# Attention with a joint block, routing and a second layer: two-strip values products, five places for bias groups, and copies at other steps

## The chip, the cores and the metric

The kernel runs on one core of a Trainium2 chip. The metric is the device time of one execution in microseconds (us). The kernel before takes 361.13 us, the median of three runs (360.67 to 361.41).

## The reference

Three layers follow one another: an attention whose scores get a bias from a small network of relative positions, a mixture of experts that sends each token to one of eight, and a gated layer. Inputs and output are 32-bit floats.

```python
B, H, S, D = 2, 8, 576, 64           # batches, heads, sequence, head width
scores = q @ k.transpose(0, 1, 3, 2) / sqrt(D)
x = log1p(abs(i - j)) / log1p(max(i, 1))
h = maximum(x[..., None] @ w1 + b1, 0)          # 32 hidden units per (i, j)
scores += (h @ w2).transpose(2, 0, 1)           # one bias plane per head, both batches share it
attn = softmax(scores) @ v
tokens = attn as 1152 rows of 512
expert = argmax(tokens @ w_gate); gate = softmax at that expert
y = gate * relu(tokens @ w1[expert]) @ w2[expert]   # at most 288 tokens per expert
h = y @ w_in                                    # 512 -> 2048
out = (h * cos(h)) @ w_out
```

## The kernel before, in words

**Attention** is cut into nine blocks of 128 query rows and each block into four steps, one for a pair of heads: 36 steps. The 576 rows of a batch are four blocks of 128 and one of 64; the two blocks of 64 (one of each batch) are worked on together as the joint block, `BOTH`, which is the fifth in the order and holds steps 16 to 19.

All engines' orders are written out by hand, in `step_of(n)`. Step n issues the score products of step n+1 (`emit_qk`, L403, into the two-bank tiles `sa` and `sb`), and in the same step VectorE adds the bias and takes the row minimum of the negated score (`emit_sum`, L411; `mn`). ScalarE takes the exponential (`emit_exp`, L420), TensorE turns it in strips of 64 (`emit_tr`, L428), ScalarE copies the turned strips out of PSUM (`emit_tev`, L451 and L454). TensorE multiplies the turned strips of step n-1 with the values (`emit_pv`, L470), and ScalarE copies that product (L480). Two steps later the product is turned back (L501, L553 in the routing part) and scaled (L508).

`emit_pv` has the values as the stationary operand, in strips of 32 columns, and the turned exponentials as the moving one, so four strips lie side by side in the array. For a block of 128 rows that is 5 times 4 matmuls with 128 moving columns. For the joint block it is 2 times 5 times 4 with 64 moving columns. The trace shows each of these matmuls as two pairs of a weight load and a matmul.

**The bias** is made in 36 groups of 16 query rows, ten (`LEAD`) ahead of the first step and one in each of the steps 0 to 25, group g = n + 10 in step n. A group is: four hidden tiles `h` (`bias_h`, L321 on VectorE or L319 on ScalarE), two half products in `bb` of four strips each (`bias_half`, L347), two evictions on ScalarE into a place `ev_t[g]` (L353), and a copy from that place to the plane of its block (`bias_out`: L328 to `keep` or `bias`, L338 to `joint`, which lies in `wi`). The second half's eviction is done at the start of the next step. The places are three buffers taken in turn, `ev_buf[g % 3]`; only groups 8 to 13 have six of their own (`ev_first`). A place is written again only when the copy out of it has landed. `h` in step 0 is all four tiles of group 10, behind the first four sums.

**SP's queue** issues nearly all copies, one after the other, in the order in which they are written: bias copies, the queries (`fetch_q`, L306), the filling of the dispatch table with rows that count for nothing (`fill_rows`, L840, at the steps `FILL_AT`), zeros into the output (`fill_out`, L843, at `OUT_AT`), and `double` (L835), which copies the joint block's bias planes of a head pair to the second batch's 64 rows, once per step from step `DOUBLE_AT` on. A `double` waits for the bias copies of groups 16 to 19.

**Routing** runs inside the steps. After the first blocks the kernel picks the expert that it works on first and, at step `SECOND_CHOICE` on VectorE behind the step's scaling, the second one (`second_choice`: L684 and the four operations of `largest`, L674 to L677). SP reads that number two steps later. From step 26 on (`PLAIN`) there are no bias groups; VectorE then does parts of the weights' widening (L757 to L763). The experts and the gated layer come after step 35.

Of the kernel before, what the change touches and what calls it, by code (L numbers as in the profile page):

```python
# [20 lines left out]
B, H, S, D = 2, 8, 576, 64  # L21
# [6 lines left out]
RW = DM + 4  # L28
# [10 lines left out]
MAGS = 28, 29, 30, 31, 33  # L39
LOWS = {28: 3, 29: 2, 30: 2, 31: 3, 32: 2, 35: 3}  # L40
ROUTE_FROM = 17
FILL_AT = 6, 7, 8, 9, 13, 14, 15, 16, 17, 18, 19
DOUBLE_AT = 10
OUT_AT = 10, 12, 12, 20, 20, 21, 21, 22, 22
SECOND_CHOICE = 27
PLAIN = 26
LATE_FROM = 32
LATE_A = {33: 1}
# [5 lines left out]
LEAD = 10  # L54
# [13 lines left out]
BOTH = B  # L68
# [38 lines left out]
def attention_moe_kernel(  # L107
    ctx: ExitStack, tc: tile.TileContext,
    qd, kd, vp, small, ttab, wg, mw1, mw2, win, wout, out, dbg=None,
# [72 lines left out]
    cut = lambda a, n: flat[:, a:a + n]  # L182
# [2 lines left out]
    base = 9 * RW + 2 * NP * 128  # L185
    lt_buf = cut(base, 128)
    ev_buf = [cut(base + 144 + S * i, S) for i in range(3)]
    ev_first = dict(zip(range(8, 14), ev_buf + [cut(a, S) for a in (6 * RW + 60, S * 3, S * 2)]))
    v13 = cut(base + 144 + 3 * S, 640)


# [77 lines left out]
    bias_a = bias_p.tile([128, H, S], F32, name="bias0")  # L269
# [12 lines left out]
    def v_of(b, p, a, n):  # L282
        for lo, hi, t in v_parts[b, p]:
            if lo <= a and a + n <= hi:
                return t[:, a - lo:a - lo + n]
# [6 lines left out]
    def fetch_k(b, p):  # L292
        Y.dma_start(out=kt[b, p], in_=kd[b, :, 2 * p:2 * p + 2, :])
# [17 lines left out]
    def bias_h(g, on_act=(), quads=(0, 1, 2, 3)):  # L311
        _, _, first = GROUPS[g]
        for j in quads:
            base = first[j]
            h = h_lead[(4 * g + j) % 12] if g < LEAD else h_buf[(4 * g + j + 4) % 8]
            win_ = tt[:, C0 - base:C0 - base + S]
            col = pst[:, 4 * g + j:4 * g + j + 1]
            if j in on_act:
                A.activation(out=h, in_=win_, func=AF.Relu, bias=col, scale=1.0)  # L319
            else:  # L320
                V.tensor_scalar(out=h, in0=win_, scalar1=col, scalar2=0.0, op0=ALU.add, op1=ALU.max)  # L321
            h_t[g, j] = h

    ev_t = {}

    def bias_part(g, a, e):
        ib, r, _ = GROUPS[g]
        Y.dma_start(out=bias_t[ib][r:128:8][:, :, a:e], in_=ev_t[g][:, a:e])  # L328

    def bias_out(g, cuts=((0, S),)):  # L330
        ib, r, _ = GROUPS[g]
        ev = ev_t[g]
        if IBN[ib] == 128:
            for a, e in cuts:
                bias_part(g, a, e)
        else:
            for rr in range(2):
                Y.dma_start(out=joint[r + rr:64:8], in_=ev[64 * rr:64 * rr + 64])  # L338
        for j in range(4):
            h_t.pop((g, j))  # L340

    def bias_half(g, half, bank=bb):
        if half == 0:
            ev_t[g] = ev_first.get(g, ev_buf[g % 3])
        cols, ps = slice(half * 288, half * 288 + 288), bank[:, :288]
        for j in range(4):
            T.matmul(out=ps[32 * j:32 * j + 32, :], lhsT=w2s, rhs=h_t[g, j][:, cols], start=True, stop=True)  # L347

        def evict():
            if (g, half) == (NG - 1, 1):  # L350
                V.tensor_scalar(out=ev_t[g][:, cols], in0=ps, scalar1=rst[:, g:g + 1], scalar2=None, op0=ALU.mult)
            else:
                A.activation(out=ev_t[g][:, cols], in_=ps, func=AF.Copy, scale=rst[:, g:g + 1])  # L353
            if g == NG - 1:
                bias_part(g, half * 288, half * 288 + 288)
            elif half == 1:
                bias_out(g)

        return evict
# [1 line left out]
    lead_t = {}  # L361

    def bias_lead(g):
        ev_t[g] = bias_a[:, g] if g < 8 else ev_first[g]
        lead_t[g] = (xb, bb) if g == 9 else (t0, t1) if g % 3 == 2 else [s_bank[1 - g % 3][:, i] for i in range(2)]
        for half in range(2):
            for j in range(4):
                T.matmul(
                    out=lead_t[g][half][32 * j:32 * j + 32, 0:288], lhsT=w2s,
                    rhs=h_t[g, j][:, 288 * half:288 * half + 288], start=True, stop=True,  # L370
                )
# [11 lines left out]
    e_t, et_t, z_t, xs_t, xn_t, rz_t = {}, {}, {}, {}, {}, {}  # L383
# [76 lines left out]

    def emit_pv(n):
        b, ib, p = steps[n]
        et = et_t[n]
        et_t.pop(n)
        for c, a, e in [(c, 64 * c, 64 * c + 64) for c in range(B)] if b == BOTH else [(b, 0, 128)]:
            xo = sum_of(n)[:, a:e]
            for j in (4, 0, 1, 2, 3):
                for i in range(4):
                    u, at_ = i // 2, 512 + 32 * i if j == 4 else 64 * (4 * (i // 2) + j) + 32 * (i % 2)
                    T.matmul(  # L470
                        out=xo[32 * i:32 * i + 32], lhsT=v_of(c, p, at_, 32),
                        rhs=et[:, 4 if j == 4 else 5 * u + j, a:e], start=(j == 4), stop=(j == 3),
                    )
        if p == 0:
            xs_t[b, ib] = xs_buf[n // NP % 2]
            xn_t[b, ib] = rows[tile_of(b, ib)]
# [184 lines left out]
    def choose():  # L661
# [24 lines left out]

        hooks[SECOND_CHOICE, "values"] = [second_choice]
        hooks[SECOND_CHOICE + 2, "start"] = [lambda: known(ix2)]

# [99 lines left out]
    def warm(n):  # L789

        for _ in range(n):
            T.matmul(out=wu[:, 0:128], lhsT=ones, rhs=ones, start=True, stop=True)
# [60 lines left out]
            fetch_k(1, 0)  # L853
    load_v(0, (2,))
    fetch_k(1, 1)
    warm(8)
    emit_sum(0, 0)
    emit_sum(0, 1)
# [6 lines left out]
    def step_of(n):  # L865

        g, nxt = RUNS.get(n), RUNS.get(n + 1)
        at_step[0] = n
        if n > 1:
            b, ib, p = steps[n - 2]  # L870
            if p == NP - 1 and n < SOONER:
                finish_block(b, ib)
                ready.append((b, ib))

        while ready and n >= ROUTE_FROM:
            tile_done(*ready.pop(0))
        while late and n < LATE_FROM and late[0][0] == -2:
            whole(late.pop(0)[1])
        if 0 < n <= PLAIN:
            emit_exp(n, 1)  # L880
        while behind:
            behind.pop(0)()
        if n in MAGS:
            early_mags.pop(0)()
        hook(n, "first")
        if n + 1 < ns:
            b, ib, p = steps[n + 1]
            j = BLOCKS.index((b, ib))
            for u in range(2):
                emit_qk(n + 1, u)  # L890
            if p == 0 and 0 < j < len(BLOCKS) - 1:
                fetch_q(*BLOCKS[j + 1])
            if n == 0:
                bias_h(g)
            emit_exp(n + 1, 0)
        if n == ns - 4:
            aux[0] = V
        hook(n, "start")
        emit_tr(n)
        if n > 1:  # L900
            emit_nat(n - 2)
        hook(n, "turned")
        emit_tev(n, 2)
        if g is not None:
            bias_half(g, 0)()
        emit_tev(n, 0)
        if n >= LATE_FROM:
            go_on(run_late(LATE_A.get(n, 0)))
        emit_tev(n, 1)
        begun = run_late(LATE_B.get(n, n < LATE_FROM))  # L910
        e_t.pop(n)
        if nxt is not None:
            bias_h(nxt, quads=(0, 1))
        go_on(begun)
        if n > 1:
            emit_nrm(n - 2)
        if nxt is not None:
            bias_h(nxt, quads=(2, 3))
        while held:
            held.pop(0)()  # L920
        for _ in range(LOWS.get(n, 0)):
            early_lows.pop(0)()
        hook(n, "values")
        if 0 < n:
            emit_rz(n - 1)
            emit_pv(n - 1)
            if PLAIN <= n < ns - 1:
                emit_exp(n + 1, 1)
            emit_xs(n - 1)
        if n == SOONER:  # L930
            b, ib, p = steps[n - 1]
            finish_block(b, ib)
            tile_done(b, ib)
        go_on(run_late(LATE_C.get(n, 0)))
        if g is not None:
            evict = bias_half(g, 1, bb if n > 1 else xb[:, 128:])
            if g == NG - 1:
                evict()
            else:
                behind.append(evict)  # L940
        made_up()
        load_step(n)
        while again and again[0][0] <= n:
            fetch_piece(again.pop(0)[1])
        if n in FILL_AT:
            i = FILL_AT.index(n)
            fill_rows(256 * i, min(256, E1 * CAP - 256 * i))
        if 0 <= n - DOUBLE_AT < NP:
            double(n - DOUBLE_AT)
        for j, at_ in enumerate(OUT_AT):  # L950
            if at_ == n:
                fill_out(j)
        hook(n, "end")
# [139 lines left out]
    b, ib, p = steps[ns - 1]  # L1093
# [454 lines left out]
```

## Time and profile before

| | us |
|---|---|
| median of three runs | 361.13 (360.67 to 361.41) |
| the profiled execution, its own time | 361.79 |
| its span, first to last instruction | 360.0 |
| TensorE busy in the span | 341.8 (95%) |
| VectorE | 293.9 (82%) |
| ScalarE | 266.8 (74%) |
| GpSimd | 37.7 (10%) |

The mean granted TensorE clock is 0.994 of 2.4 GHz; the page's row of slices shows the full clock up to the last slice. Busy time of TensorE counts matmuls whose ends are modelled, so the shares say little of a single stage. What matters is which engine the others wait for in each step: a gap on TensorE, and what ended it.

### The profile page before, as it was taken

Reading aid. Unit: us, or ns where it says so; the run is one execution under the profiler, and the core shown is the slowest. Engines: PE = TensorE matmul, PEld = TensorE weight load, DVE = VectorE, ACT = ScalarE, POOL = GpSimd, SP = SyncE. Lnnn points to the kernel's source line nnn. Section 1 sums busy time; section 2 is a strip of 40 time slices with the busy share of each in tenths; the row PEclk is TensorE's granted clock in tenths of the full one; section 3 lists DMA queues with packets and bytes.
Section 4 is the critical chain, followed back from the end, with each engine's and each line's share of the span. In section 5 each row is a group of like instructions: output and inputs, shape, how many; then the busy total and the mean of one; then the engine's idle time right before and its main releaser. Section 6 shows DMA issues by size and latency. Waiting matters only on the chain. (4 is left out here: it accounts for less than half of the span.)

```text
span 360.0 us, 11244 instructions
## 1 busy us (share of the span) xinstructions
PE 341.8 (95%) x4459; PEld 272.8 (76%) x4459; DVE 293.9 (82%) x771; ACT 266.8 (74%) x627; POOL 37.7 (10%) x89
## 2 busy tenths in 40 slices
PE   7989999999989999898999999999999999999991
PEld 6346777775656777686789999968898898898880
DVE  5988889898869886988799999887997887876760
ACT  6768999987978898898943597387777667666560
POOL 3000001101001420110007112100000000000023
PEclk9999999999999999999999999999999999999997
DMA  7799966679976687799238698943243242110003
GB/s 234 203 246 278 251 168 194 203 157 258 277 244 190 205 247 192 249 258 310 90 109 309 167 353 280 295 157 119 66 121 107 91 131 73 58 62 0 2 28 117
DMA packets 47023, 63.89 MB, mean 177 GB/s; under 512 B 5772, under 2 KB 30476, under 8 KB 46962
## 3 DMA queue, kind: packets, MB, share of 16 engines
q1 hardware_dynamic: 45666, 60.24, 57.8%
q0 software_dynamic: 1152, 2.48, 1.9%
q8 instruction: 37, 0.61, 0.7%
q10 hardware_dynamic: 144, 0.36, 0.3%
q14 instruction: 24, 0.20, 0.2%
HBM read 41.08 MB, written 11.47 MB: 146 GB/s over the span
## 5 line engine op out<-in xcount | busy, mean ns | idle before, releaser
L420 ACT ACTIVATE e<-e,mn 128x576 f32<-128x576 f32 x72 | 56.2, 781 | 14.8 <-DVE mn L411 14.8
L321 DVE TENSOR_SCALAR h<-tt,sml 128x576 f32<-128x576 f32 x122 | 57.0, 513 | 0.1
L451 ACT ACTIVATE et<-t 128x512 f32<-128x512 f32 x72 | 38.7, 593 | 0.0
L347 PE MATMUL bb<-h,sml 128*32 128x288 f32 x400 | 35.6, 412 | 1.1 <-DVE h L321 0.6
L428 PEld LDWEIGHTS t<-ident,e 64*128 64x128 f32 x576 | 24.3, 139 | 8.9 <-issue 1.8
L403 PE MATMUL sb<-k,q 64*128 64x288 f32 (+1 forms) x160 | 27.0, 449 | 0.4 <-DVE lp L556 0.3
L353 ACT ACTIVATE wo<-bb,sml 128x288 f32<-128x288 f32 x49 | 24.7, 504 | 3.5 <-PE bb L347 2.1
L428 PE MATMUL t<-ident,e 64*128 64x64 f32 x576 | 26.1, 225 | 1.1 <-ACT e L420 0.8
L1281 PE MATMUL t<-yh,s1h 128*128 128x352 f32 (+1 forms) x88 | 26.8, 305 | 0.0
L1281 PE MATMUL t<-yh,s1l 128*128 128x352 f32 (+1 forms) x88 | 26.6, 303 | 0.0
L1281 PE MATMUL t<-yl,s1h 128*128 128x352 f32 (+1 forms) x88 | 26.5, 302 | 0.0
L1392 DVE TENSOR_TENSOR tn<-tn,kn 128x608 f32<-128x608 f32 (+2 forms) x18 | 13.0, 722 | 15.8 <-ACT kn L1389 15.7
L470 PE MATMUL sa<-et,wi 128*32 128x128 f32 (+1 forms) x800 | 23.0, 260 | 1.6 <-issue 1.6
L1402 ACT ACTIVATE gh<-tn 128x608 fp32r<-128x608 f32 (+2 forms) x18 | 11.8, 656 | 17.0 <-DVE tn L1399 17.0
L403 PE MATMUL sa<-k,q 64*128 64x288 f32 (+1 forms) x160 | 23.8, 406 | 0.0
L470 PEld LDWEIGHTS sa<-et,wi 128*32 128x32 f32 x800 | 19.5, 110 | 3.9 <-issue 1.7
L403 PEld LDWEIGHTS sb<-k,q 64*128 64x128 f32 (+1 forms) x160 | 10.5, 174 | 14.7 <-issue 6.0
L1018 PE MATMUL hp<-xh,s1h 128*128 128x288 f32 x64 | 19.5, 305 | 0.0
L1377 PE MATMUL hp<-s2h,gh 128*128 128x512 f32 x48 | 19.1, 399 | 0.0
L1021 ACT ACTIVATE hh<-hp 128x288 fp32r<-128x288 f32 x16 | 6.5, 409 | 17.0 <-PE hp L1018 17.0
L1377 PE MATMUL hp<-s2l,gh 128*128 128x512 f32 x48 | 19.0, 396 | 0.0
L1377 PE MATMUL hp<-s2h,gl 128*128 128x512 f32 x48 | 18.9, 394 | 0.0
(308 smaller groups left out, 999.9 us busy)
## 6 DMA issues: line engine op xcount, KB each, us to landing
keep<-win SPq DMA_DIRECT2D x16, 512.0 KB
keep<-wout SPq DMA_DIRECT2D x16, 512.0 KB
w1r<-mw SPq DMA_DIRECT2D x12, 512.0 KB
w2r<-mw SPq DMA_DIRECT2D x12, 512.0 KB
disp<-wo SPq DMA_DIRECT2D x10, 516.0 KB
bias<-wo SPq DMA_DIRECT2D x15, 288.0 KB
q<-qd SPq DMA_DIRECT2D x8, 512.0 KB
k<-kd SPq DMA_DIRECT2D x8, 288.0 KB
```

The source lines that it names most:

```text
L321: V.tensor_scalar(out=h, in0=win_, scalar1=col, scalar2=0.0, op0=ALU.add, op1=ALU.max)
L347: T.matmul(out=ps[32 * j:32 * j + 32, :], lhsT=w2s, rhs=h_t[g, j][:, cols], start=True, stop=True)
L353: A.activation(out=ev_t[g][:, cols], in_=ps, func=AF.Copy, scale=rst[:, g:g + 1])
L403: T.matmul(out=ps[a:e, half, 0:HS], lhsT=qt[b, ib][rows_, h, a:e], rhs=kt[c, p][rows_, u, :], start=True, stop=True)
L420: A.activation(out=e_t[n][:, u], in_=e_t[n][:, u], func=AF.Exp, scale=-1.0, bias=mn_t[n][:, u:u + 1], accum_out=z_t[b, ib][:, h:h + 1],)
L428: T.transpose(ps, src[half], ident[half, half])
L451: A.activation(out=et_t[n][:, 0:8, 64 * g:64 * g + 64], in_=halves[g], func=AF.Copy)
L470: T.matmul(out=xo[32 * i:32 * i + 32], lhsT=v_of(c, p, at_, 32), rhs=et[:, 4 if j == 4 else 5 * u + j, a:e], start=(j == 4), stop=(j == 3),)
L1018: T.matmul(out=ps, lhsT=a[g % 3][:, k], rhs=x[:, k], start=(k == 0 and i == 0), stop=(k == 3 and i == 2))
L1281: done.append(T.matmul(out=sums(f, i), lhsT=w[f % 3][:, k], rhs=ya[k][x][:, o0 + a:o0 + e], start=(k == 0 and n == 0), stop=(k == 3 and n ...
L1377: T.matmul(out=oacc[t][rows_of(t)], lhsT=x, rhs=b[f % 3], start=(f == 0 and n == 0), stop=(f == 15 and n == 2))
L1392: V.tensor_tensor(out=tn, in0=tn, in1=kn, op=ALU.subtract)
```

## The change

It has five parts.

1. `emit_pv` takes the joint block's values in two strips of 64 columns in place of four of 32: 20 matmuls a step in place of 40, each writing 64 rows.
2. Groups 14 to 26 take their places from five buffers in turn, `ev_buf` and two regions of `wo` that groups 12 and 13 used alone.
3. The copies are issued at other steps: one filling goes from step 13 to 10, three zero copies from steps 10, 12, 12 to 8, 9, 11, and the four `double`s from steps 10 to 13 to steps 12 to 15.
4. Two of group 10's four hidden tiles are made ahead of the first sum, one of them on ScalarE.
5. The second choice is made in step 26 in place of 27. SP's order is as before there.

```diff
-FILL_AT = 6, 7, 8, 9, 13, 14, 15, 16, 17, 18, 19
-DOUBLE_AT = 10
-OUT_AT = 10, 12, 12, 20, 20, 21, 21, 22, 22
-SECOND_CHOICE = 27
+FILL_AT = 6, 7, 8, 9, 10, 14, 15, 16, 17, 18, 19
+DOUBLE_AT = 12
+OUT_AT = 8, 9, 11, 20, 20, 21, 21, 22, 22
+SECOND_CHOICE = 26
...
-    ev_first = dict(zip(range(8, 14), ev_buf + [cut(a, S) for a in (6 * RW + 60, S * 3, S * 2)]))
+    ev_more = [cut(S * i, S) for i in (3, 2)]
+    ev_at = dict(zip(range(8, 14), ev_buf + [cut(6 * RW + 60, S)] + ev_more))
+    ev_at.update({g: (ev_buf + ev_more)[(g - 14) % 5] for g in range(14, 27)})
...
-            ev_t[g] = ev_first.get(g, ev_buf[g % 3])
+            ev_t[g] = ev_at.get(g, ev_buf[g % 3])
...
-        et = et_t[n]
-        et_t.pop(n)
+        et = et_t.pop(n)
+        w = 64 if b == BOTH else 32
...
-                for i in range(4):
-                    u, at_ = i // 2, 512 + 32 * i if j == 4 else 64 * (4 * (i // 2) + j) + 32 * (i % 2)
+                for i in range(128 // w):
+                    u, at_ = w * i // 64, 512 + w * i if j == 4 else 64 * (4 * (w * i // 64) + j) + w * i % 64
                     T.matmul(
-                        out=xo[32 * i:32 * i + 32], lhsT=v_of(c, p, at_, 32),
+                        out=xo[w * i:w * i + w], lhsT=v_of(c, p, at_, w),
...
     fetch_k(1, 1)
+    bias_h(LEAD, on_act=(0,), quads=(0, 1))
     warm(8)
...
             if n == 0:
-                bias_h(g)
+                bias_h(g, quads=(2, 3))
```

Two lines are added above the sums' code, so L411 is L413 after the change, and so on.

VectorE at the first sums (the last evictions of the lead groups, the sums of steps 0 and 1, and group 10's hidden tiles h_97 to h_100), before:

```order
L376 TENSOR_SCALAR wo<-bb,sml 128x288
L411 ISA e,mn<-sb,keep 128x576
L411 ISA mn 128x1
L411 ISA e,mn<-sa,keep 128x576
L411 ISA mn 128x1
L411 ISA e,mn<-sb,keep 128x576
L411 ISA mn 128x1
L411 ISA e,mn<-sa,keep 128x576
L411 ISA mn 128x1
L321 TENSOR_SCALAR h_97<-tt,sml 128x576
L321 TENSOR_SCALAR h_98<-tt,sml 128x576
L321 TENSOR_SCALAR h_99<-tt,sml 128x576
```

The same place after the change:

```order
L378 TENSOR_SCALAR wo<-bb,sml 128x288
L323 TENSOR_SCALAR h_98<-tt,sml 128x576
L413 ISA e,mn<-sb,keep 128x576
L413 ISA mn 128x1
L413 ISA e,mn<-sa,keep 128x576
L413 ISA mn 128x1
L413 ISA e,mn<-sb,keep 128x576
L413 ISA mn 128x1
L413 ISA e,mn<-sa,keep 128x576
L413 ISA mn 128x1
L323 TENSOR_SCALAR h_99<-tt,sml 128x576
L323 TENSOR_SCALAR h_100<-tt,sml 128x576
```

One tile has moved ahead of the four sums, and h_97 has gone to ScalarE, where it stands ahead of the first exponential.

SP's queue from the last joint copies (`wi<-wo`) on, with the doubles (`wi<-wi`), the zero copies (`out_dram<-wo`), the fillings (`disp<-wo`) and the next block's bias copies (`keep<-wo`), before:

```order
L338 DMA wi<-wo 8x8x576 x2
L835 DMA wi<-wi 64x2x576
L843 DMA out_dram<-wo 128x512
L328 DMA keep<-wo 16x8x576
L306 DMA q_91<-qd 128x8x64 x2
L835 DMA wi<-wi 64x2x576
L328 DMA keep<-wo 16x8x576
L835 DMA wi<-wi 64x2x576
L843 DMA out_dram<-wo 128x512 x2
L328 DMA keep<-wo 16x8x576
L840 DMA disp<-wo 256x1x516
L835 DMA wi<-wi 64x2x576
```

After the change:

```order
L340 DMA wi<-wo 8x8x576 x2
L842 DMA disp<-wo 256x1x516
L330 DMA keep<-wo 16x8x576
L308 DMA q_91<-qd 128x8x64 x2
L845 DMA out_dram<-wo 128x512
L330 DMA keep<-wo 16x8x576
L837 DMA wi<-wi 64x2x576
L330 DMA keep<-wo 16x8x576
L837 DMA wi<-wi 64x2x576
L330 DMA keep<-wo 16x8x576
L842 DMA disp<-wo 256x1x516
L837 DMA wi<-wi 64x2x576
```

The first double now stands behind two of the next block's bias copies, where it stood ahead of all of them.

VectorE from step 26 to the first sum of step 28 (scaling L508, the slot numbers L631, the second choice L684 to L677, the sums L411), before, where all of it is in step 27:

```order
L508 TENSOR_TENSOR wo<-xb,rz 128x128
L631 SCALAR_TENSOR_TENSOR sl<-idxf,ov 128x1
L684 SCALAR_TENSOR_TENSOR cnt<-gone,cnt 128x8
L674 MAX top_74<-cnt 128x8
L675 MAX_INDEX ix_81<-top_74,cnt 128x8
L676 CAST some<-ix_81 128x1
L677 TENSOR_SCALAR hot<-eio,some 128x8
L489 TENSOR_SCALAR rz<-z 128x4
L490 RECIPROCAL rz<-rz 128x4
L411 ISA e,mn<-sb,bias_156 128x576
```

After the change the five operations stand behind step 26's scaling:

```order
L510 TENSOR_TENSOR wo<-xb,rz 128x128
L686 SCALAR_TENSOR_TENSOR cnt<-gone,cnt 128x8
L676 MAX top_74<-cnt 128x8
L677 MAX_INDEX ix_81<-top_74,cnt 128x8
L678 CAST some<-ix_81 128x1
L679 TENSOR_SCALAR hot<-eio,some 128x8
L413 ISA e,mn<-sb,bias_156 128x576
```

They now stand ahead of the sums that step 27 issues, and between the slot numbers and the sums that step 28 issues only the pair L489 and L490 is left.

## Rows read from the trace of the kernel before

**Rows 1.** Windows: us, then busy (count) of PE, PEld, DVE, ACT, POOL; clock; DMA share; GB/s.

```profile
22.00:178.00 156.00, 149.01 (x3057) 107.35 (x3057) 133.08 (x433) 135.31 (x370) 16.13 (x52) 1.00 0.82 226
178.00:353.00 175.00, 173.05 (x1200) 154.59 (x1198) 144.68 (x302) 114.88 (x230) 17.11 (x18) 1.00 0.41 132
```

**Rows 2.** Timeline, step 0: start, length, group, count, [idle before <-what ended it].

```profile
22.38 0.75 DVE L411 CUSTOM_DVE_ANT_0 e<-sb,keep 128x576 f32<-128x576 f32 x1
...
23.17 0.78 ACT L420 ACTIVATE e<-e,mn 128x576 f32<-128x576 f32 x1 [1.21 <-DVE mn L411]
...
25.36 3.52 DVE L321 TENSOR_SCALAR h<-tt,sml 128x576 f32<-128x576 f32 x8
...
25.93 1.72 PE L347 MATMUL bb<-h,sml 128*32 128x288 f32 x7 [0.55 <-DVE h L321]
```

**Rows 3.** SP's queue: one of its waits (total, times, longest) and one issue of the timeline.

```profile
SPq L835 <- DMA wi<-wo: 4.2, 1, 4.2
...
79.61 0.60 SPq L328 DMA_DIRECT2D keep<-wo  x1
```

**Rows 4.** Timeline, step 14: the first eviction of group 24, and TensorE behind it.

```profile
87.78 0.50 ACT L353 ACTIVATE wo<-bb,sml 128x288 f32<-128x288 f32 x1 [1.37 <-DMA keep<-wo]
...
88.33 0.69 PE L347 MATMUL bb<-h,sml 128*32 128x288 f32 x8 [0.55 <-ACT wo L353]
```

**Rows 5.** Timeline of TensorE in the joint block's values products, steps 17, 18 and 20.

```profile
100.29 0.96 PE L470 MATMUL sa<-et,wi 128*32 128x64 f32 x56
102.82 0.54 PE L470 MATMUL sa<-et,wi 128*32 128x64 f32 x24 [1.56 <-issue]
...
106.56 0.77 PE L470 MATMUL sa<-et,wi 128*32 128x64 f32 x40
...
107.70 0.67 PE L347 MATMUL bb<-h,sml 128*32 128x288 f32 x8
...
116.90 0.59 PE L470 MATMUL sa<-et,wo 128*32 128x64 f32 x27 [0.50 <-issue]
```

**Rows 6.** Page: busy times; instruction queue (packets, MB, share). Window between the two stalls.

```profile
PE 341.8 (95%) x4459; PEld 272.8 (76%) x4459; DVE 293.9 (82%) x771; ACT 266.8 (74%) x627; POOL 37.7 (10%) x89
...
q8 instruction: 37, 0.61, 0.7%
...
102.80:116.41 13.61, 13.59 (x383) 9.10 (x384) 11.31 (x40) 11.45 (x32) 1.59 (x6) 1.00 0.61 173
```

**Rows 7.** Timeline of TensorE: products of 128 columns (steps 15, 26), score products in 64x64 tiles (18).

```profile
91.53 1.27 PE L470 MATMUL sa<-et,v 128*32 128x128 f32 x40
92.63 0.67 PE L347 MATMUL bb<-h,sml 128*32 128x288 f32 x8
...
103.78 0.71 PE L403 MATMUL sb<-k,q 64*64 64x288 f32 x8
104.31 0.67 PE L403 MATMUL sa<-k,q 64*64 64x288 f32 x8
...
141.68 1.30 PE L470 MATMUL bb<-et,v 128*32 128x128 f32 x40
142.91 0.76 PE L403 MATMUL sb<-k,q 64*128 64x288 f32 x4
```

**Rows 8.** Timeline, steps 27 and 28: VectorE, then TensorE.

```profile
143.71 0.76 DVE L411 CUSTOM_DVE_ANT_0 e<-sb,bias 128x576 f32<-128x576 f32 x1 [0.73 <-PE sb L403]
...
146.85 0.16 DVE L631 SCALAR_TENSOR_TENSOR sl<-idxf,ov 128x1 int32<-128x1 f32 x1 [0.44 <-POOL ov L624]
146.93 0.16 DVE L684 SCALAR_TENSOR_TENSOR cnt<-gone,cnt 128x8 f32<-128x8 f32 x1
...
147.93 0.16 DVE L489 TENSOR_SCALAR rz<-z 128x4 f32<-128x4 f32 x1
...
148.22 0.73 DVE L411 CUSTOM_DVE_ANT_0 e<-sb,bias 128x576 f32<-128x576 f32 x1
...
149.02 0.18 PE L695 MATMUL sb<-srun,ones 128*128 128x8 bf16 x1 [0.71 <-DVE mn L411]
```

More of the change, by code (lines that the diff above doesn't have):

```diff
@@ L363, in bias_lead @@
     def bias_lead(g):
-        ev_t[g] = bias_a[:, g] if g < 8 else ev_first[g]
+        ev_t[g] = bias_a[:, g] if g < 8 else ev_at[g]
         lead_t[g] = (xb, bb) if g == 9 else (t0, t1) if g % 3 == 2 else [s_bank[1 - g % 3][:, i] for i in range(2)]
```

## The prediction

> **What bounds the kernel now.** I read the busy times of two stretches first. In attention (22 to 178 us) TensorE is busy 149.01 of 156.00 us, behind it 173.05 of 175.00 us [rows 1]. VectorE and ScalarE have 20 us or more to spare in attention. So TensorE sets the pace, and what a change can win there is TensorE's gaps, about 7 us, or work taken from TensorE. The second stretch has 2 us of gaps; a shift of attention's end should therefore reach the end of the kernel whole. The granted clock is 1.00 in both stretches.
>
> Then I went through TensorE's timeline for gaps, and four of those in attention stand where the change has an edit: 0.55 us in step 0, behind VectorE's hidden tiles [rows 2]; 0.55 us in step 14, behind a ScalarE eviction that waited 1.37 us for a copy [rows 4]; 1.56 and 0.50 us inside the joint block's values products, where the releaser is only "issue" [rows 5]; and 0.71 us in step 28, behind VectorE's sum [rows 8]. Together 3.87 us.
>
> **Part 4, two hidden tiles ahead of the sums.** Before, eight tiles take 3.52 us [rows 2], about 0.43 us each, and group 10's four begin at 25.36, behind four sums. One of the two moved tiles goes to ScalarE, which is idle for 1.21 us there [rows 2] and has room for it. The other stays on VectorE, ahead of the sums: they, and the exponentials behind them, start 0.43 us later, for the first sum follows the eviction ahead of it without a gap. Behind the sums two tiles are left in place of four, 0.86 us less. The last of the four is ready 0.86 - 0.43 = 0.43 us sooner, and TensorE's products of the group wait for it. I take **-0.43 us**; the bounds are 0 (the later exponentials give it back) and -0.55 us (the whole gap).
>
> **Parts 2 and 3, places and copies.** The eviction at 87.78 is the first half of group 24 and takes the place that group 21 used. That group's copy was issued at 79.61, and the wait ended 8.2 us later [rows 3, 4]. On SP it stood behind doubles, the first of which kept the queue blocked for 4.2 us for the joint copies [rows 3]. With five places group 24 takes the place of group 19, whose copy leaves two steps earlier and, in the new order, ahead of all doubles. The wait has no cause left. I take TensorE's gap, **-0.55 us**, not ScalarE's 1.37, since TensorE sets the pace; bounds 0 and -1.37. What moves on SP: one filling, three zero copies and four doubles, each an issue of about 0.6 us [rows 3]. They add at most two issues to a step from 8 to 11. I cost them at nothing: nobody waits for fillings or zeros inside attention, and the cover is SP's idle time between its issues. If it were gone, bias copies would leave later, which with five places has two steps more of slack. The doubles come two steps later. Each then leaves at the end of a step, and the sum that reads it is issued three steps on, so two whole steps lie between; a step lasts some 4.5 us (from the sum at 143.71 to the next at 148.22 [rows 8]), two of them 9.0 us. A flight as long as the 8.2 us above just fits.
>
> **Part 1, strips of 64.** Three things change.
>
> (a) The stalls. TensorE stops 56 pairs (load and matmul) into step 17's 80, and again inside step 20's. Between the two it runs 383 pairs, 766 instructions [rows 6]. The page counts 2 x 4459 instructions on TensorE and 37 packets on one instruction queue [rows 6], so some 241 counted instructions per packet; 766 is 3 x 255. So the stalls are three packets apart, and I read them as TensorE running out of fetched instructions where 160 of them go in 1.14 us (106.56 to 107.70 [rows 5]). The new strips make that 80 in about the same time, as in the plain steps, where I found no such gap. I take -2.06 us; bounds 0 and -2.06.
>
> The Trainium skill, "Runtime: NRT & Kernel Launch", section Instruction fetch mechanics, says that instructions come in 16 KiB blocks of 256 and that crossing a block is mostly hidden. The trace agrees on the distance and not on the hiding; by the page these stalls would have another cause, which is the first rival.
>
> (b) The products themselves. Four strips of 32 share a wave: plain steps take 1.10 us for 10 waves of 128 columns (91.53 to 92.63 [rows 7]), 0.86 ns a column; the joint step takes 1.14 us for 20 waves of 64, 0.89 ns a column. So columns set the time, not the number of instructions. Two strips of 64 are again 20 waves of 64 columns, if both run at once. The nearest row is the score products in 64x64 tiles: eight in 0.53 us (103.78 to 104.31), four at once, 288 columns, 0.92 ns a column [rows 7]. I take no change; the near bounds are -0.1 and +0.2 us over four steps. The far ones are worked out under the rivals.
>
> (c) The array's shape. Ahead of and behind these products stand bias products in strips of 32. In plain steps the values products are followed by more strips of 32 after 1.10 us [rows 7]; in step 26, where the scores in another shape follow, the same 40 take 1.23 us (141.68 to 142.91 [rows 7]). A change of shape costs about 0.12 us. Strips of 64 add one behind the products in four steps and one ahead in step 17 (in the others another shape stands ahead already): 5 x 0.12 = +0.6 us; bounds 0 and +1.0.
>
> The Trainium skill, "TensorEngine Tiling (Array Packing)", section Key Properties, says that any change of tiling mode drains TensorE. No row here shows 32 to 64 columns; by the page it drains like the others and part 1 wins 1.46 us, and were it not so it would be 2.06.
>
> Part 1 is -2.06 + 0.6 = **-1.46 us**.
>
> **Part 5, the second choice.** In step 27 its five operations run from 146.93 to 147.93 on VectorE, and the next sum starts without a gap at 148.22 [rows 8]; TensorE then waits 0.71 us for it. Without them the sum starts 1.0 us earlier. In step 26 they stand ahead of a sum that had 0.73 us of idle time before it [rows 8]: the remaining 0.2 to 0.3 us delay that sum. It has nobody waiting on TensorE at once, and VectorE itself waits 0.44 us for GpSimd a little later. Step 28's sum then comes about 0.8 us earlier, and TensorE's gap goes: **-0.7 us**; bounds 0 and -1.0. SP's order is unchanged, and its number is ready earlier.
>
> **The sum** is -0.43 - 0.55 - 1.46 - 0.7 = **-3.1 us**. Against the profiled execution's own 361.79 us that is 358.7. That execution is 0.66 us above the median of the runs, 361.13, so the median after should be **358.0 us**. A measurement of this kernel tells about 0.2%, 0.7 us, from no change.
>
> **Rivals.**
> - The stalls stay, or come back elsewhere. For it: the fetched blocks' borders shift by 320 instructions for all later steps, and the row says only "issue". Against: the distance of three packets, and no such gap in the plain steps. Then 2.06 us is not won: -1.08 us, 360.05 us.
> - The small waits are only passed on. In steps 28 to 35 all three engines wait for each other, and step 0's sums are later. If half of the three small gains (1.68 us) is lost, the time is 358.9 us.
> - The instructions, not the columns, set the products' pace. At the old 14.3 ns a pair (1.14 us / 80), 40 pairs would take 0.57 us, 2.3 us less over four steps: 355.7 us. Against: the two rates per column above.
> - Slower: two strips of 64 do not run at once. Then 40 waves of 57 ns take 2.28 us a step, 4.6 us more over four steps, and the sum is +1.4 us: 362.5 us. It decides from where a joint step's products take 1.14 + 3.1 / 4 = 1.9 us. Against it stand the 64x64 tiles, which run four at once.
> - The copies don't do what they should: a joint sum waits for its double, or another copy is late. Each microsecond of lateness costs one; from 3.1 us on the kernel is slower.
>
> **How the numbers follow.** The forecast has 0.57, the stalls that stay 0.17, the waits passed on 0.13, the faster products 0.05, the serial strips 0.04, late doubles 0.04. The forecast alone, with its near bounds, reaches from 357.2 to 358.8. The range takes in the waits passed on and the stalls that stay, and a little of the faster products: 356.7 to 360.2 us; some 0.15 is left out. Faster by over 0.2%, that is below 360.4: the first four cases but for the worse half of some, 0.86. Within 0.2%: 0.08. Slower: 0.06.
>
> **What would show it.** In the profile after: no gap on TensorE ahead of group 10's products larger than 0.1 us; no ScalarE wait for a copy at an eviction; the joint block's products without an "issue" gap, 1.1 to 1.2 us for 40 pairs, and bias products behind them about 0.1 us later; no wait of 0.7 us in step 28, and VectorE's idle time in step 26 to 27 gone. The attention's end comes about 3.1 us earlier, and the rest keeps its length. The forecast is wrong if the gaps go and others of the same size open behind them, if an "issue" gap stands in another step, or if a joint step's products take 1.5 us or more.

## The result and the profile after

The changed kernel takes 358.84 us, the median of 20 runs (357.96 to 360.82); the kernel before takes 362.11 us beside it, also of 20 (360.67 to 366.02). The ratio is **0.9897 (0.9878 to 0.9917)**: faster by 1.0%, where 0.9914 was forecast (358.0 of 361.13); 358.84 lies inside the forecast range of 356.7 to 360.2. The profiled execution has a span of 357.9 us and a time of its own of 359.65 us.

The windows of the changed kernel, as [rows 1], and two lines of its page, as [rows 6]:

```profile
22.00:178.00 156.00, 151.25 (x2945) 109.67 (x2945) 135.29 (x436) 138.77 (x377) 16.26 (x53) 1.00 0.81 226
178.00:353.00 175.00, 170.69 (x1153) 152.57 (x1151) 142.41 (x298) 112.59 (x225) 18.50 (x19) 1.00 0.41 135
```

```profile
PE 342.0 (96%) x4299; PEld 273.4 (76%) x4299; DVE 293.8 (82%) x770; ACT 267.7 (75%) x628; POOL 37.6 (11%) x89
...
q8 instruction: 35, 0.57, 0.7%
```

TensorE's gaps in the window of attention fell from 7.0 to 4.75 us, and the granted clock is 1.00 as before. On the whole page there are 160 pairs of load and matmul fewer and two packets fewer on the instruction queue.

The timeline of the changed kernel at the place of [rows 2], VectorE and then TensorE:

```profile
22.65 0.51 DVE L323 TENSOR_SCALAR h<-tt,sml 128x576 f32<-128x576 f32 x1
23.08 0.75 DVE L413 CUSTOM_DVE_ANT_0 e<-sb,keep 128x576 f32<-128x576 f32 x1
...
26.06 2.66 DVE L323 TENSOR_SCALAR h<-tt,sml 128x576 f32<-128x576 f32 x6
...
26.01 1.48 PE L349 MATMUL bb<-h,sml 128*32 128x288 f32 x7
```

One tile stands ahead of the first sum, six operations are left behind the sums in place of eight, and the 0.55 us gap ahead of TensorE's products is gone. At the place of [rows 4] the eviction has no idle time before it, and so TensorE none behind it. ScalarE there:

```profile
87.46 0.50 ACT L355 ACTIVATE wo<-bb,sml 128x288 f32<-128x288 f32 x1
```

TensorE in the joint block's products, as [rows 5]:

```profile
99.96 0.40 PE L546 MATMUL xb<-wo,wgs 128*32 128x128 f32 x8
100.30 1.39 PE L472 MATMUL sa<-et,wi 128*64 128x64 f32 x40
101.61 0.69 PE L349 MATMUL bb<-h,sml 128*32 128x288 f32 x8
...
105.01 0.80 PE L472 MATMUL sa<-et,wi 128*64 128x64 f32 x20
105.64 0.75 PE L472 MATMUL sa<-et,v 128*64 128x64 f32 x20
106.33 0.69 PE L349 MATMUL bb<-h,sml 128*32 128x288 f32 x8
```

No "issue" gap is left in the joint block. A step's 40 pairs take 1.31 us to the next product (100.30 to 101.61), where 80 took 1.14.

The second choice, as [rows 8], VectorE and then TensorE:

```profile
145.50 0.16 DVE L633 SCALAR_TENSOR_TENSOR sl<-idxf,ov 128x1 int32<-128x1 f32 x1 [0.44 <-POOL ov L626]
...
145.87 0.73 DVE L413 CUSTOM_DVE_ANT_0 e<-sb,bias 128x576 f32<-128x576 f32 x1
...
146.70 0.17 PE L697 MATMUL sb<-srun,ones 128*128 128x8 bf16 x1
```

The sum follows the slot numbers after 0.37 us, not 1.37, and the 0.71 us gap is gone. But TensorE has a gap that was not there before, six steps into attention:

```profile
46.17 0.28 PE L430 MATMUL t<-ident,e 64*128 64x64 f32 x3
47.48 0.65 PE L430 MATMUL t<-ident,e 64*128 64x64 f32 x13 [1.04 <-issue]
```

**Where the time went** is best read from VectorE's first sums, one per step, since their starts mark the steps in every kernel. Interval k runs from the first sum of step k-1 to that of step k; a gap that the prediction puts into step n stands in interval n + 2 (step 28's, just behind the sum that ends interval 29). Us, worked out from the starts in the timelines:

| interval | before | after | after, profiled again |
|---|---|---|---|
| start of sum 0 | 22.38 | 23.08 | 23.32 |
| 2 (hidden tiles) | 5.20 | 4.35 | 4.35 |
| 7 | 4.31 | 5.51 | 4.31 |
| 16 (group 24's eviction) | 5.22 | 4.46 | 4.47 |
| 17 to 22 (joint block) | 29.03 | 26.96 | 26.96 |
| 28 + 29 (second choice) | 7.88 | 7.27 | 7.28 |
| 30 | 3.96 | 3.95 | 4.25 |

The other intervals agree within 0.07 us. Of sum 0's 0.70 us, 0.43 is the moved tile; the lead's last eviction started 0.27 later (21.95 and 22.22), and sum 0 also moved by 0.36 in a kernel whose code up to there is the one before (a1 below). By its parts the change won 0.42 + 0.76 + 2.07 + 0.61 = 3.86 us in this execution, lost 1.20 in interval 7 and 0.27 at the start, and stood 2.35 us ahead at the last sum. The span is only 2.1 us shorter: from the last step's first sum to the end it is 188.2 us before and 188.5 after. In the second profile of the changed kernel that stretch takes 190.0 us, and over all profiles of this document 188.2 to 190.9. So the prediction's "the rest keeps its length" holds here to within about 2 us only, and a gain below that is read from the intervals, not from the span of one profile.

### The profile page after: what moved, and what is told of

It reads as the page before. It is cut to its first block, busy times and chain, and to the rows that moved or that the text cites. A ratio compares the mean times of both kernels' runs of the same rounds, so it can differ in the third digit from the quotient of the medians.

```text
span 357.9 us, 10923 instructions
## 1 busy us (share of the span) xinstructions
PE 342.0 (96%) x4299; PEld 273.4 (76%) x4299; DVE 293.8 (82%) x770; ACT 267.7 (75%) x628; POOL 37.6 (11%) x89
## 5 line engine op out<-in xcount | busy, mean ns | idle before, releaser
L472 PEld LDWEIGHTS sa<-et,wi 128*32 128x32 f32 (+1 forms) x700 | 19.7, 114 | 2.4 <-DVE mn L413 1.5
L1021 PE MATMUL hp<-xh,s1l 128*128 128x288 f32 x64 | 18.9, 295 | 0.0
```

Source lines behind the costliest of these rows:

```text
L472: T.matmul(out=xo[w * i:w * i + w], lhsT=v_of(c, p, at_, w), rhs=et[:, 4 if j == 4 else 5 * u + j, a:e], start=(j == 4), stop=(j == 3),)
L1021: T.matmul(out=ps, lhsT=a[g % 3][:, k], rhs=x[:, k], start=(k == 0 and i == 0), stop=(k == 3 and i == 2))
```

## The experiments

Beside the experiments the kernel before took 363.5 to 364.0 us, so ratios to it are compared. Each experiment has one profile, of one of its runs; those of a1, u2 and u3 are of the slowest run each. Two questions were open.

- **The stalls.** Theory F: TensorE waits for instructions, at borders of the blocks in which they are fetched. Its rival: something in these products themselves, or in their data, stops it.
- **The copy wait.** Theory A: the five places end it. Theory B: the copies' new steps end it alone.

**u1: strips of 32 put back, the rest as changed.**

```diff
-        w = 64 if b == BOTH else 32
+        w = 32
```

> The changed kernel with the joint block's values in four strips of 32 again, all else as changed. Theory (fetched instructions run out in the joint steps): an issue gap of 0.5 to 1.6 us stands inside the values products of at least one of steps 17 to 20, the products take 1.14 us a step where they run through, and the time is 0.9 to 1.5 us above the changed kernel's 358.84 us, about 360.0. Rival (the two-strip form itself gives nothing, the stalls were chance): no issue gap in the joint steps, and 0.6 to 0.9 us below the changed kernel.

Ratio 0.9941 (0.9914 to 0.9968): 0.44% above the changed kernel's, some 1.6 us, a little over the 0.9 to 1.5 expected. TensorE's timeline, and two windows:

```profile
100.57 0.40 PE L546 MATMUL xb<-wo,wgs 128*32 128x128 f32 x8
100.79 0.96 PE L472 MATMUL sa<-et,wi 128*32 128x64 f32 x56
102.36 0.54 PE L472 MATMUL sa<-et,wi 128*32 128x64 f32 x24 [0.61 <-issue]
...
116.45 0.59 PE L472 MATMUL sa<-et,wo 128*32 128x64 f32 x27 [0.49 <-issue]
```

```profile
48.15:102.30 54.15, 53.60 (x1148) 38.36 (x1148) 47.36 (x150) 48.81 (x134) 4.18 (x15) 1.00 0.81 223
102.30:116.40 14.10, 13.59 (x383) 9.11 (x384) 11.98 (x46) 12.07 (x33) 1.60 (x6) 1.00 0.67 196
```

The stalls are back behind the same 56th pair and with the same 27 left. This execution also has the gap of interval 7 (1.32 us, ending at 48.15), and the windows between the three hold 1148 and 383 pairs: 9 x 127.6 and 3 x 127.7. The places where the stalls stand, about 128 pairs or a multiple of it apart, are called borders below, and all borders of one kernel its grid. Intervals 17 to 22 take only 27.63 us here, against 29.03 before: in this execution the stalls of the joint block are smaller (0.61 and 0.49 us, and none hidden) though the strips are those of before.

**p: 64 small matmuls ahead of everything, in the kernel before.** It only shifts what follows by 64 pairs.

```diff
+    for _ in range(64):
+        T.matmul(out=wu[:, 0:8], lhsT=ones, rhs=ones[:, 0:8], start=True, stop=True)
```

> The kernel before with 64 small matmuls of 8 columns more at the start, 128 instructions; it computes the same. Theory (fetched blocks of instructions): an issue gap, where there is one, stands 64 pairs earlier in the order than before, or blocks of 128 pairs from there: in step 17 not behind the 56th of 80 pairs but ahead of the products, or in the 120th pair after the old place. Rival (the stall belongs to these products' operands): it stands behind the 56th pair again. The time itself says little, since the start is longer.

One run, 364.67 us. TensorE's timeline, and the window between the two gaps:

```profile
101.55 0.43 PE L544 MATMUL xb<-wo,wgs 128*32 128x128 f32 x8 [0.53 <-issue]
101.79 1.30 PE L470 MATMUL sa<-et,wi 128*32 128x64 f32 x80
...
107.75 0.28 PE L428 MATMUL sb<-ident,e 64*128 64x64 f32 x2 [2.39 <-issue]
```

```profile
101.50:107.70 6.20, 3.81 (x128) 2.59 (x128) 3.63 (x12) 3.52 (x10) 0.00 (x0) 1.00 0.80 256
```

The first gap stands ahead of the eight routing products: 8 + 56 = 64 pairs earlier in the program than before. The products that used to stall run through in one piece, and the next gap comes 128 pairs on, in transposes. The rival falls: the stall belongs to a place in the instruction stream. That TensorE waits there for instructions is inferred, from this shift and from the distance of 128 pairs; no row names a fetch.

**a1: part 1 alone, in the kernel before.**

```diff
-                for i in range(4):
+                for i in range(128 // w):
...
-                        out=xo[32 * i:32 * i + 32], lhsT=v_of(c, p, at_, 32),
+                        out=xo[w * i:w * i + w], lhsT=v_of(c, p, at_, w),
```

> The kernel before with the joint block's values in two strips of 64 alone. Theory: no issue gap in steps 17 to 20, products and shape changes 0.2 us longer a step, and 1.0 to 1.5 us below the kernel before. Rival (the stall is where the instructions' borders fall, and moves to another step): an issue gap elsewhere in attention, and 0 to 0.5 us below.

Ratio 0.9969 (0.9943 to 0.9996): a third of what all parts bring, some 1.1 us, as the theory said; the gap elsewhere is the rival's. ScalarE and TensorE in its timeline:

```profile
88.94 0.50 ACT L353 ACTIVATE wo<-bb,sml 128x288 f32<-128x288 f32 x1 [1.97 <-DMA keep<-wo]
...
104.15 0.51 ACT L353 ACTIVATE wo<-bb,sml 128x288 f32<-128x288 f32 x1
...
89.49 0.69 PE L347 MATMUL bb<-h,sml 128*32 128x288 f32 x8 [1.15 <-ACT wo L353]
...
105.57 0.71 PE L403 MATMUL sa<-k,q 64*64 64x288 f32 x8 [1.13 <-ACT wo L353]
```

No gap named "issue" is left in the joint block, yet intervals 17 to 22 take 28.99 us, as long as before. The copy wait grew from 1.37 to 1.97 us, and there is a gap of 1.13 us at 105.57. Its releaser reads ScalarE, but that eviction was over at 104.66, 0.9 us sooner. What the gap is, the next run shows.

**u3: five places, copies at their old steps**, and **u23: three places, copies at their old steps.**

```diff
-FILL_AT = 6, 7, 8, 9, 10, 14, 15, 16, 17, 18, 19
-DOUBLE_AT = 12
-OUT_AT = 8, 9, 11, 20, 20, 21, 21, 22, 22
+FILL_AT = 6, 7, 8, 9, 13, 14, 15, 16, 17, 18, 19
+DOUBLE_AT = 10
+OUT_AT = 10, 12, 12, 20, 20, 21, 21, 22, 22
```

u23 has this and the diff of u2, below.

> The changed kernel with the copies at the old steps, five places. Theory A (the places alone end the wait): no ScalarE wait for a copy, and the same time within 0.3 us. Theory B (the new steps are needed): a wait of 0.5 us or more on TensorE in steps 12 to 16, 359.4 us.

> The changed kernel with three places and the copies at the old steps. Both theories: the gap of 0.55 us in step 14 comes back, and the time is 0.5 to 0.9 us above 358.84, about 359.5. If it is the same, the gap of the profile before was chance.

Ratios 0.9922 (0.9891 to 0.9953) and 0.9934 (0.9906 to 0.9963). TensorE and ScalarE in u3's timeline, and a window of u3:

```profile
98.29 0.52 PE L472 MATMUL sa<-et,wo 128*32 128x128 f32 x10 [0.75 <-issue]
...
105.59 0.72 PE L405 MATMUL sa<-k,q 64*64 64x288 f32 x8 [0.85 <-ACT wo L355]
...
104.45 0.51 ACT L355 ACTIVATE wo<-bb,sml 128x288 f32<-128x288 f32 x1
```

```profile
98.25:105.55 7.30, 6.44 (x128) 3.83 (x128) 4.38 (x14) 5.40 (x15) 0.00 (x0) 1.00 0.97 292
```

The gap at 105.59 stands exactly 128 pairs behind the "issue" gap at 98.29. So it is a fetch stall too, whatever its row names. This execution has three more, at 40.42, 48.15 and 166.08 us, each a whole number of blocks away. In u23 the same two stand at 98.07 (1.26 us) and 104.81 (0.31), with 128 pairs between; in its profile ScalarE's copy wait is back as well, but interval 16 is only 0.23 us longer for it, not the 0.5 us and more that was expected:

```profile
87.91 0.50 ACT L354 ACTIVATE wo<-bb,sml 128x288 f32<-128x288 f32 x1 [0.84 <-DMA keep<-wo]
```

```profile
47.10:98.03 50.93, 49.69 (x1020) 35.28 (x1020) 44.76 (x142) 45.40 (x125) 4.19 (x15) 1.00 0.80 202
```

From its stall in interval 7 to the one at 98.07 are 1020 pairs, 8 x 127.5.

**u2: three places, copies at their new steps.**

```diff
-    ev_at.update({g: (ev_buf + ev_more)[(g - 14) % 5] for g in range(14, 27)})
```

> The changed kernel with three places for groups 14 on again, copies at the new steps. Theory A (the places are what ended the wait in step 14): ScalarE waits for a copy at an eviction and the time is 0.5 us above 358.84, about 359.4. Theory B (the copies' new steps alone would have ended it, since SP is no longer held by a double ahead of them): no such wait, same time within 0.2 us.

Ratio 0.988 (0.9849 to 0.991), and no ScalarE wait for a copy at any eviction; interval 16 takes 4.47 us. Theory B holds as far as one profile goes: the copies' new steps are enough, and the places add nothing that shows. u3 has no such wait either, so the five places alone would also do. The wait's size is a matter of the execution: all four profiles with three places and the old steps have it, with 1.37 us before, 1.97 in a1, 0.84 in u23 and 0.55 in p, where interval 16 takes 4.47 us as if there were none; none of the other ten profiles has it. On the same chip u2 took 359.98 us (359.35 to 360.75), u3 361.06 (360.47 to 363.33) and u23 362.20 (360.57 to 362.92), so the old steps do cost time, and in the profiles it is lost to fetch stalls.

The new steps are not free in every execution: in u2 and in q (below) the first sum of step 8 waits 0.71 and 0.48 us for a copy, and interval 8 takes 4.98 and 4.75 us in place of 4.49. The changed kernel's two profiles have 4.55 and 4.49. Whether the moved copies cause it was not tested.

**u4: part 4 undone**, **u5: the second choice in step 27 again.**

```diff
-    bias_h(LEAD, on_act=(0,), quads=(0, 1))
...
-                bias_h(g, quads=(2, 3))
+                bias_h(g)
```

```diff
-SECOND_CHOICE = 26
+SECOND_CHOICE = 27
```

> The changed kernel with all four hidden tiles of group 10 behind the first sums again. Theory (group 10 is late by two tiles less one): TensorE has a gap of about 0.5 us ahead of group 10's products, and the time is 0.43 us above 358.84, 359.3. Rival (the later exponentials give it back): same within 0.15 us.

> The changed kernel with the second choice in step 27 again. Theory: TensorE's gap of 0.7 us in step 28 is back, and the time is 0.6 us above 358.84 (1.00 us won in step 28 less 0.39 us lost in step 27 in the profile), 359.45. Rival (passed on in the steps after 28): same within 0.15 us.

Ratios 0.9898 (0.9838 to 0.9959) and 0.9894 (0.9837 to 0.995): gains of 0.4 and 0.6 us are below what these runs can tell, so the profiles decide. TensorE's timeline in u4, then in u5:

```profile
26.42 1.72 PE L349 MATMUL bb<-h,sml 128*32 128x288 f32 x7 [0.55 <-DVE h L323]
```

```profile
147.74 0.18 PE L697 MATMUL sb<-srun,ones 128*128 128x8 bf16 x1 [0.71 <-DVE mn L413]
```

Each brings its own gap back, to the hundredth, and with it interval 2 (5.20 us) and intervals 28 + 29 (3.38 + 4.51); in u5 interval 30 is back at 3.96 us too.

**best: the second choice in step 25.**

```diff
-SECOND_CHOICE = 26
+SECOND_CHOICE = 25
```

> The changed kernel with the second choice in step 25, where VectorE was idle for 1.20 us behind step 25's scaling. Theory (it costs nothing where VectorE is idle): the 0.39 us that step 27 lost goes, 358.4 to 358.5 us. Rival (the loss has another cause, or step 25 loses as much): 358.8 us.

Ratio 0.9866 (0.9813 to 0.9918). Intervals 28 and 29 take 3.38 and 3.51 us: the changed kernel's 0.39 us in interval 28, where the five operations stand ahead of a sum, are gone as well. That is the fastest point of all kernels here, though its interval covers the changed kernel's. TensorE's timeline, later in attention:

```profile
161.81 0.95 PE L472 MATMUL bb<-et,wi 128*32 128x128 f32 x25 [1.12 <-issue]
```

Interval 33, in which this stall stands, takes 4.68 us, as in kernels without it: there VectorE is the one waited for.

**d: two strips everywhere**, and **q: best, with two strips also in steps 4 and 5.**

```diff
-        w = 64 if b == BOTH else 32
+        w = 64
```

```diff
+        w = 64 if b == BOTH or n in (4, 5) else 32
```

> The changed kernel with the values in two strips of 64 in all 36 steps. Theory (columns set the pace, a change of the array's shape costs 0.12 us): from step 27 on, where other shapes stand on both sides anyway, the products take their old 1.23 us within 0.1; in steps 1 to 16 a step is 0.15 to 0.3 us longer, some 25 such steps, so 4 to 6 us slower than the changed kernel, and no issue gap in any step. Rival (instructions set the pace, or two strips do not run at once): products of steps 27 on at half or at twice the time.

> The second choice in step 25 and two strips of 64 also for the values products of steps 4 and 5, in which the stall ahead of step 7's sum is fed. Theory (fetched instructions): no issue gap ahead of step 7's sum; 0.3 to 0.5 us for the two products' shape changes against a stall of 0.7 to 1.3 us that came in five of eight profiles; 0.2 us below the kernel with the choice in step 25 alone, 1.3 to 1.5% below the kernel before. Rival: the gap moves to step 8 and the kernel is 0.4 us slower than that one.

Ratios 1.004 (1.0019 to 1.006) and 0.9911 (0.9877 to 0.9946), neither with an "issue" gap. d is 4.7 us slower than the changed kernel beside it (365.29 and 360.60), as expected; q won 0.9% where 1.3 to 1.5% was expected, and since best has no stall ahead of step 7's sum either, q doesn't show that its strips prevent one. TensorE in d's timeline:

```profile
143.66 1.31 PE L472 MATMUL bb<-et,v 128*64 128x128 f32 x20
144.90 0.76 PE L405 MATMUL sb<-k,q 64*128 64x288 f32 x4
```

Between neighbours of other shapes, 20 pairs of 128 columns in two strips take 1.24 us where 40 in four took 1.23 [rows 7]: the columns set the pace. Ahead of step 27 nearly every step is 0.15 to 0.3 us longer in d, where two strips put a change of shape that four strips of 32 don't have, and in q the two steps cost 0.29 and 0.26 (the second beside the wait for a copy; d has 0.15 there). So in these runs fewer instructions paid only where a border stalled.

**r: the changed kernel again.**

> The changed kernel once more, with a second profile, as the measure for the other three on the same chip. Theory (the stall of 1.04 us ahead of step 7's sum is chance, from a full DMA queue): it may be there or not, the steps without an issue gap last as in its first profile within 0.05 us, and the ratio to the kernel before is 0.990 again, within 0.003.

Ratio 0.9911 (0.988 to 0.9942). It has no "issue" gap at all, and interval 7 takes 4.31 us. The stall there is a matter of the execution: of the 11 profiles whose TensorE runs the same instructions up to there, 5 have it (after, u1, u3, u23, u5). All five are of kernels with part 4, and none of the three without it (before, a1, u4) has it; that may be chance, and it stays open. In u5 a smaller stall follows at the next border, and its interval 8 is 0.39 us longer.

## Why the prediction was right, point by point

| part | forecast | intervals of the profile |
|---|---|---|
| 4, hidden tiles | -0.43 | -0.42 |
| 2 and 3, copies | -0.55 | -0.76 |
| 1, two strips (with part 3, below) | -1.46 | -2.07 |
| 5, second choice (interval 30 apart, below) | -0.7 | -0.61 |
| sum | -3.1 | -3.86 |
| a stall in interval 7, and the start | none | +1.47 |

The medians differ by 3.27 us, near the 3.1 of the sum. That they are so near is partly luck: two terms were too small, one was too large in most executions, and the first two rivals came true in part; these errors have opposite signs.

**Part 4** came as worked out.

**Parts 2 and 3.** The gain was sized by TensorE's gap, and the interval gave 0.21 us more, in this execution; from the other kernels with the old places and steps it would have been 0 (p), 0.23 (u23) and 1.35 (a1). The sentence that failed is "With five places group 24 takes the place of group 19 [...] The wait has no cause left": true as far as u3 shows, but not needed, since u2 does without. The prediction costed the copies' moves "at nothing"; by u2 they are enough for this wait, and as far as the profiles go they also act on the fetching (below).

**Part 1 (a)**, the stalls, is the term that was mis-sized: 2.06 us by the idle time in [rows 5], about 2.8 by the program's pace. A row's idle time begins at the modelled end of the matmuls ahead, up to a few tenths of a microsecond after the last one was issued. In step 17 the products took 2.89 us to the next ones (100.29 to 103.18), 1.75 more than 1.14. In step 20 ten pairs begin at 116.02 and the next come at 116.90; at 14.3 ns each that is 0.74 us of waiting. And a third stall showed no gap at all. TensorE's timeline before, step 16:

```profile
95.64 1.51 PE L470 MATMUL sa<-et,wo 128*32 128x128 f32 x38
...
97.67 0.72 PE L403 MATMUL sb<-k,q 64*64 64x288 f32 x8
```

and after:

```profile
95.87 1.28 PE L472 MATMUL sa<-et,wo 128*32 128x128 f32 x40
...
97.56 0.71 PE L405 MATMUL sb<-k,q 64*64 64x288 f32 x8
```

The same work took 2.03 us and then 1.69, 0.34 less; u3's stall behind the 28th of these 40 shows that a border lies there. 1.75 + 0.74 + 0.34 = 2.83 us.

**Part 1 (b) and (c)**, the products and the change of shape, were +0.6 and measured about +0.84: 4 x 0.18 (1.31 and 1.32 for 1.14), and +0.12 on entering step 17, where the routing products ahead take 0.34 us to the next start, against 0.22 in u1. With -2.83 that makes -1.99 of the -2.07 in the table.

**Why two strips help** is what the prediction had, in a sharper form. The borders are still there, and the next one behind step 16's products comes 128 pairs on, as before. What changed is how soon TensorE gets to it. From about the 28th of those 40 on, windows of before and of after, both with 136 matmuls on record:

```profile
96.40:101.10 4.70, 4.70 (x136) 3.11 (x130) 3.62 (x11) 4.11 (x11) 0.00 (x0) 1.00 1.10 342
```

```profile
96.64:102.75 6.11, 6.11 (x136) 3.85 (x130) 4.61 (x14) 5.82 (x17) 0.00 (x0) 1.00 1.03 305
```

With strips of 32 TensorE was through in 4.70 us (0.34 of it the hidden stall) and then stood; with strips of 64 it takes 6.11 and finds the next block there. The time from one border to the next block, where a stall shows it, was 6.2 us before (96.62, where the first product behind the border starts, to 102.82), 5.1 in u1, 6.2 in p, 6.7 in u23, 7.3 in u3 and 7.5 in a1. The six profiles with two strips, this grid and the copies at their new steps (after, r, u2, u4, u5, best) pass the border without a stall, and the three with the copies at their old steps (a1, u3, u23) stall there. So part 3 made part 1 pay: alone, part 1 won 0.3%. And the 2.07 us of the joint block are not part 1's alone: intervals 17 to 22 take 29.03 us before, 28.98 with the strips alone (a1), 27.63 with all but the strips (u1) and 26.96 with all, each in one execution. Why the copies' steps matter to the fetch is argued only: instructions come through a DMA queue too [rows 6], and the DMA engines are full in this stretch (share 1.10 and 1.03). But that share does not tell the stalls apart: from the border on it is 1.01 to 1.05 in the six profiles without one, and 1.09 in a1, 0.97 in u3 and 1.01 in u23. So the cause on the copies' side stays open.

The Trainium skill, "Runtime: NRT & Kernel Launch", section Instruction fetch mechanics, gives blocks of 256 instructions and calls the crossing mostly hidden. The counts here, 127.5 to 128 pairs, agree with the block. "Mostly" holds as well: the 3057 pairs of attention before [rows 1] cross some 24 borders, and three stalled.

**Part 5** won 0.61 us by intervals 28 and 29: 1.00 in the one, and 0.39 lost in the other, where 0.2 to 0.3 was forecast. About half of it is given back one interval later. Interval 30 is 3.95 us here, but 4.20 to 4.26 in the nine other profiles with the choice moved, and 3.96 in all four with it in step 27. In those nine VectorE waits 0.16 to 0.22 us behind step 28's sums for the small product that TensorE makes there (`sb<-srun,ones`), and in the other five it doesn't. VectorE in the second profile:

```profile
146.49 0.17 DVE L699 CUSTOM_DVE_ANT_0 cnt<-sb,gone 128x8 f32<-128x8 f32 x1 [0.21 <-PE sb L697]
```

Before, TensorE waited for VectorE at this place. So the second rival, the waits passed on, holds for part 5: about 0.3 us are left of its 0.61.

**The rivals.** "The stalls stay, or come back elsewhere" (0.17) was half right: not in the joint block, but one of 1.04 us stood at another border of the same grid. An "issue" gap in another step was one of the prediction's own signs of being wrong, and it came, in one of two profiles. The rows of before could not show it, because that border did not stall in that execution. The serial strips are refuted by 1.31 us a step where 1.9 was the point of decision, the instructions' pace by d.

## To carry to other kernels

Where "issue" gaps on a busy engine stand whole numbers of the same count of instructions apart, and move with instructions put in ahead, read them as fetch stalls: count pairs between gaps to tell it, and distrust a releaser that had ended long before the gap did. What counted here was how soon the engine reached the next border (4.70 us stalled, 6.11 did not) and at which steps the copies stood; the larger instructions paid little without the moved copies. Size a gain by the distance between fixed points of the step, not by the idle time of the row, which here missed a quarter of it, and look a few steps further on for what is given back.

## What the runs showed of the hardware that was not expected

- Fetch stalls of 0.3 to 2.4 us, at borders a whole number of blocks of 127 to 128 pairs apart. Whether a given border stalls differs between executions of the same kernel: 1.04 us at 47.48 in one profile of the changed kernel, none in the other.
- A fetch stall can hide behind modelled matmul ends (0.34 us without a gap before, some 0.3 in u5, one block behind its stall of interval 7) or under another engine's name (0.85 us "ScalarE" in u3).
- A change between strips of 32 and of 64 costs TensorE some 0.12 to 0.17 us. Halving the number of instructions wins nothing by itself: in d, 20 pairs take 1.24 us where 40 took 1.23.
